# Four of eight experts in one wide pass, picked from 33 programs, and their output transposed back by DMA

## The chip, the cores and the metric

The kernel runs on one core of one Trainium2 chip. The metric is the device time of one execution in microseconds, the median of several runs of the same program. The profile comes from one further execution; its span, from the first to the last instruction, is a little shorter than the device time (270.0 us beside 271.8 us for that run). TensorE (PE in the profile, with its weight loads as PEld), VectorE (DVE), ScalarE (ACT), GpSimd (POOL) and SyncE (SP) have queues of their own [...]; 16 DMA engines move data beside them.

## What is computed

A block of the kind of Mamba 2 (chunked state space attention) gives 3072 tokens of 256 numbers. Each token then goes to one of eight experts. Only the second part, cut to its core, is touched by the change:

```python
def _moe_ref(x, w_gate, w1, w2):           # x 3072x256, w1 8x256x1024, w2 8x1024x256
    logits = x @ w_gate
    expert_idx = np.argmax(logits, axis=1)
    ...                                     # probs = softmax(logits)
    gate_w = probs[np.arange(N), expert_idx]
    for e in range(E):
        mask = expert_idx == e
        xe = x[mask]
        h = np.maximum(xe @ w1[e], 0.0)
        out[mask] = gate_w[mask, None] * (h @ w2[e])
```

With the inputs of the reference the experts get 372, 343, 418, 417, 336, 365, 415 and 406 tokens. The kernel may not know these counts; it finds them on the chip.

## The kernel before

Everything is fp32, with tokens along the free axis in the first layer. The routing puts each token's row (256 numbers, 8 logits, its number: `W` = 265) into `x_hbm`, where every expert has a stretch of `NR` rows. The first 17 of 24 token tiles are placed during the attention part, the last seven (`late`) between the matmuls of the experts. Rows that no token fills have to be zero and carry a token number that is out of range, so that their output is dropped: `empty(e)` writes them from `zrows`.

The expert part has two passes. The first takes 256 rows (`CA`) of each of the eight experts. The second takes what is beyond them, experts in pairs: 128 rows of each, and up to 64 more of each in one half tile. For the second pass the largest count of the pair chooses one of five programs, 128 + 16c columns wide:

```python
def up(xT, w, f, n, pp, step=CA):                    # first layer, one of 8 blocks of h
    p = pp.tile([128, 512], FP32, name="h_ps", tag="h", bufs=4)
    for i in range(0, n, step):
        for t in range(KT):                          # KT = 2
            c = t * F + f * 128
            nc.tensor.matmul(p[:, i:min(i + step, n)], lhsT=w[:, c:c + 128], rhs=xT[:, t, i:min(i + step, n)],
                             start=(t == 0), stop=(t == KT - 1))
    return p[:, 0:n]

def m_y(e, hT, xs, gt, mo, pp, between=None, scalar=True, last=False):   # second layer, 128 tokens
    p = pp.tile([128, DM], FP32, name="y_ps", tag="y", bufs=2)
    for f in range(FT):                              # FT = 8
        nc.tensor.matmul(p, lhsT=hT[:, f], rhs=w_sb[e][1][:, f * DM:f * DM + DM], start=(f == 0),
                         stop=(f == FT - 1))
        ...
    put(p, xs, gt, mo, scalar, last)                 # scale by the gate, send rows to out by their numbers

for v in range(E // 2):                              # second pass
    ...
    for c in tc.Switch(cls[v], 5, f"p{v}"):
        for i in range(2):
            m_h(2 * v + i, pr[v]["xT"][i], pr[v]["hT"][i], 128 + 16 * c, pp)
        if c:
            m_half(v, mo, pp)                        # the two halves share one 128-row result
    send(yh, pr[v]["xh"][:, 0])
    ...                                              # hint of the next switch, rows of the next pair
    for i in range(2):
        m_y(2 * v + i, ...)
```

The hidden layer comes out of `up` with its features on partitions and goes into `m_y` as the stationary operand, so that the output rows have tokens on partitions and can be scattered. The first layer needs the rows transposed. VectorE splits the fp32 rows into 16-bit halves (`halves`, L651), a DMA transposes them (L653), and VectorE joins them again (`words`, L658):

```python
def halves(tiles):
    ...
    for i, xs in enumerate(tiles):
        f = xs.bitcast(U16).rearrange("p (j c) -> p c j", c=2)
        for t in range(KT):
            nc.vector.tensor_copy(pl[:, i, :, t], f[:, :, HB * t:HB * t + 128])
    tt = ea.tile([128, TA + 1, 2, KT, 128], U16, name="plT", bufs=2)[:, 0:n]
    nc.sync.dma_start_transpose(out=tt..., in_=pl...)
    return tt
```

Weights of all eight experts (2 MB each: `w1` and `w2`) have buffers of their own and are loaded once, in order, by SyncE's queue, ahead of their use; they stay for the second pass.

## Time and profile before

| | |
|---|---|
| device time, median of 3 runs | 271.53 us (270.83 to 271.98) |
| span of the profile | 270.0 us |
| first matmul of the experts | 83.2 us |
| first pass of the eight experts | 83.2 to 194.6 us |
| second pass, four pairs | 194.6 to 262.8 us |
| last seven tiles placed by GpSimd | 119.7 to 149.3 us |
| rows of the second pass first read | 167.2 us |
| DMA | 43.57 MB, mean 161 GB/s |

The page shows for each engine its busy time, then the span in 40 slices of 6.75 us with the busy share in tenths. A row of a group names the line of the source, the engine, the operation and the tiles (output<-input), how often it ran, its busy time and mean duration; behind the second bar stands the time for which its engine had been idle before it, and what ended that. The chain of waits follows the work that ended last backwards from the end, step by step, to what released each. Where a step is a matmul, the stretch from its start to the next is TensorE's own pace. SPq is SyncE issuing DMAs: their data move later. Every source matmul in fp32 shows as two instructions, so 64 instructions `h_ps` are the 32 matmuls of a pair.

### The profile page before, as it was taken

What the parts mean: (1) busy time and instruction counts of PE and PEld (TensorE: products, weight loads), DVE (VectorE), ACT (ScalarE), POOL (GpSimd) and SP (SyncE); (2) the same over time, 40 slices, a digit from 0 to 9 for tenths busy, and PEclk for the clock granted to TensorE, in tenths of its full rate; (3) what the DMA queues carried; (4) which work ended last, traced back from release to release, by engine and by line L of the source; (5) the groups of instructions that cost most, each with busy time, mean ns of one, the idle gap of its engine ahead of it and who ended that gap; (6) DMA issues with size and microseconds to landing.
All of it is one profiled execution on the core that took longest, in us unless ns stands there. A gap on an engine that the chain in (4) does not pass through costs nothing.

```text
span 270.0 us, 7603 instructions
## 1 busy us (share of the span) xinstructions
PE 252.9 (94%) x3044; PEld 213.7 (79%) x3067; DVE 110.7 (41%) x358; ACT 104.5 (39%) x304; POOL 87.0 (32%) x171
## 2 busy tenths in 40 slices
PE   8799898999997999999999999999999999999990
PEld 2577677677776888888888888888998978989770
DVE  4889887888854240421211111233225115321010
ACT  6958574655543423223232323141050520604200
POOL 5666875866720002025504120202211102121021
PEclk9999999999999999999999999999999999999996
DMA  6956767671434899949695959533330601401010
GB/s 182 374 172 171 228 199 236 165 247 51 135 118 101 212 367 310 384 177 294 236 256 202 279 199 335 130 91 78 103 85 9 94 4 30 90 6 40 2 35 28
DMA packets 29715, 43.57 MB, mean 161 GB/s; under 512 B 16203, under 2 KB 19917, under 8 KB 27984
## 3 DMA queue, kind: packets, MB, share of 16 engines
q1 hardware_dynamic: 27152, 36.32, 45.4%
q0 software_dynamic: 2496, 6.41, 7.1%
q8 instruction: 36, 0.59, 0.9%
q14 instruction: 31, 0.25, 0.3%
HBM read 29.10 MB, written 10.73 MB: 147 GB/s over the span
## 4 chain that ended last, share of the span: by engine, by line
PE 82%; DVE 5%; DMA 4%; issue 4%; POOL 2%; ACT 1%; POOLq 0%; ACTq 0%; DVEq 0%
PE h_ps L685 33%; PE y_ps L720 30%; PE y L176 5%; PE rows_ps L176 4%; PE g L176 3%; PE A L176 3%; PE yh_ps L731 3%; DVE L L359 2%; DMA x_hbm<-rows,pos 1%; DMA xs<-x_hbm 1%; DMA az<-in_az_dram 1%; DMA ct<-in_CT_dram 1%; DVE M L386 1%; PE rank L176 1%; DVE S L431 1%
## 5 line engine op out<-in xcount | busy, mean ns | idle before, releaser
L685 PE MATMUL h_ps<-xT,w 128*128 128x256 f32 (+3 forms) x516 | 90.3, 334 | 0.6 <-ACT xT L641 0.5
L685 PEld LDWEIGHTS h_ps<-xT,w 128*128 128x128 f32 x516 | 81.3, 190 | 8.2 <-ACT xT L641 0.7
L720 PE MATMUL y_ps<-w,hT 128*128 128x256 f32 x384 | 84.9, 380 | 0.0
L720 PEld LDWEIGHTS y_ps<-w,hT 128*128 128x128 f32 x384 | 72.6, 190 | 10.5 <-issue 0.8
L696 ACT ACTIVATE hT<-h_ps 128x256 f32<-128x256 f32 (+3 forms) x128 | 43.3, 339 | 60.8 <-PE h_ps L685 53.1
L711 POOL DMA_INDIRECT out_dram<-yo,xs x24 | 23.7, 988 | 91.1 <-ACT yo L703 64.7
L553 POOL DMA_INDIRECT x_hbm<-rows,pos x24 | 24.4, 1015 | 20.6 <-DMA x_hbm<-zrows 13.3
L359 DVE TENSOR_TENSOR_SCAN L<-abc,ident 128x512 f32<-128x512 f32 x24 | 29.1, 1213 | 0.0
L651 DVE COPY pl<-xs 128x256 uint16<-128x256 uint16 x44 | 10.4, 298 | 43.8 <-DMA xs<-x_hbm 43.7
L658 DVE COPY xT<-plT 128x512 uint16<-128x512 uint16 (+1 forms) x30 | 10.6, 415 | 33.6 <-DMA plT<-pl 27.8
L703 ACT ACTIVATE yo<-y_ps,gate 128x256 f32<-128x256 f32 x14 | 6.6, 474 | 39.4 <-PE y_ps L720 24.5
L386 DVE TENSOR_TENSOR M<-g,L 128x512 f32<-128x512 f32 x24 | 16.5, 687 | 5.6 <-PE g L176 5.1
L176 PE MATMUL rows_ps<-turn,yT 128*128 128x136 f32 x96 | 15.4, 283 | 3.5 <-issue 2.7
L705 DVE TENSOR_SCALAR yo<-y_ps,gate 128x256 f32<-128x256 f32 x10 | 4.8, 482 | 29.3 <-PE y_ps L720 29.3
L176 PE MATMUL g<-ctm,bt 32*64 32x128 f32 x384 | 16.3, 280 | 0.5 <-ACT ctm L293 0.4
L176 PEld LDWEIGHTS rows_ps<-turn,yT 128*128 128x128 f32 x96 | 14.5, 192 | 1.3 <-issue 0.4
L711 POOL DMA_INDIRECT out_dram<-yh,xh x4 | 3.9, 978 | 35.7 <-ACT yh L733 23.9
L470 ACT COPY rows<-rows_ps 128x264 f32<-128x264 f32 x24 | 9.1, 380 | 13.5 <-PE rows_ps L176 10.9
L176 PE MATMUL y<-M,xn 64*32 64x64 f32 x768 | 12.9, 223 | 1.2 <-issue 1.2
L457 ACT COPY yT<-y 128x256 f32<-128x256 f32 x24 | 8.9, 372 | 12.2 <-PE y L176 10.2
L176 PEld LDWEIGHTS g<-ctm,bt 32*64 32x64 f32 x384 | 10.4, 131 | 3.2 <-ACT ctm L293 0.9
L366 POOL TENSOR_TENSOR bs<-bn,L 128x128 f32<-128x128 f32 x22 | 9.0, 410 | 11.1 <-DVE L L359 10.0
(132 smaller groups left out, 203.3 us busy)
## 6 DMA issues: line engine op xcount, KB each, us to landing
w<-in_w_dram SPq DMA_DIRECT2D x13, 1024.0 KB
x_hbm<-zrows SPq DMA_DIRECT2D x8, 463.8 KB
xn<-in_x_dram SPq DMA_DIRECT2D x12, 256.0 KB
w<-in_w_dram SPq DMA_DIRECT2D x12, 256.0 KB
xs<-x_hbm SPq DMA_DIRECT2D x8, 265.0 KB
ct<-in_CT_dram SPq DMA_DIRECT2D x6, 256.0 KB
bt<-in_BT_dram SPq DMA_DIRECT2D x6, 256.0 KB
bn<-in_B_dram SPq DMA_DIRECT2D x6, 256.0 KB
```

Of the source, the lines that this page charges most:

```text
L176: i = nc.tensor.matmul(out, lhsT=lhsT, rhs=rhs, **kw)
L359: nc.vector.tensor_tensor_scan(out=s["L"].rearrange("p h i -> p (h i)"), data0=s["abc"], data1=ident8.rearrange("p h i -> p (h i)"), initi ...
L366: nc.gpsimd.tensor_tensor(out=bs[n % 2], in0=gr[n // CG]["B"][:, n % CG].rearrange("p (h m) -> p h m", h=8), in1=bc(st[n]["L"][:, :, CH - ...
L386: nc.vector.tensor_tensor(out=s["M"].rearrange("p (s v u) i -> p s v (u i)", s=2, v=2), in0=s["g"][:, :, 0:256].rearrange("p v (s f) -> p ...
L470: nc.scalar.copy(out=rt[g][:, k - R0[g], 0:DM + E], in_=p)
L553: s_ = nc.gpsimd.indirect_dma_start(out=x_hbm[:, :], out_offset=bass.IndirectOffsetOnAxis(ap=pos[:, k:k + 1], axis=0), in_=rt[grp[k]][:, k ...
L651: nc.vector.tensor_copy(pl[:, i, :, t], f[:, :, HB * t:HB * t + 128])
L658: nc.vector.tensor_copy(xT.bitcast(U16).rearrange("p t (j c) -> p c t j", c=2), tt)
L685: nc.tensor.matmul(p[:, i:min(i + step, n)], lhsT=w[:, c:c + 128], rhs=xT[:, t, i:min(i + step, n)], start=(t == 0), stop=(t == KT - 1))
L696: nc.scalar.activation(hT[:, f, 0:n], p, func=ACT.Relu)
L711: s_ = nc.gpsimd.indirect_dma_start(out=out[:, :], out_offset=bass.IndirectOffsetOnAxis(ap=xs[:, TOK:TOK + 1].bitcast(I32), axis=0), in_=y ...
L720: nc.tensor.matmul(p, lhsT=hT[:, f], rhs=w_sb[e][1][:, f * DM:f * DM + DM], start=(f == 0), stop=(f == FT - 1))
```

## The change

Experts 0 to 3 keep their two passes. Experts 4 to 7 get one pass over all their rows, up to 512 (`CP`), by a program of the width that the count asks for, in steps of 8 from 256 to 512: 33 programs (`NCP`) for each of four experts. The aim is to spend no columns on rows that only fill tiles. So that the width of both layers can follow the count, the second layer has the weights stationary and the tokens streaming; its result has features on partitions, and a DMA transpose turns it back. The one-pass experts stand between the layers of the others, so that transposes and loads have a whole layer of matmuls beside them. Since a one-pass expert needs all its rows, all tokens are placed at the start of the expert part, and the zero rows behind the tokens (`empty_last`) are written once the final counts are known. The one-pass experts share two sets of weight buffers.

```diff
+EP = 4
+CP = 512
+NCP = (CP - CA) // 8 + 1
-NR = N + 128
+NR = N + CP
+    def empty_last(e):
+        r = nc.values_load(nk[0:1, E + 1 + e:E + 2 + e], engines=[ENG.SP], ...)
+        d = nc.sync.dma_start(out=x_hbm[ds(r + e * NR, CP), :]..., in_=zrows)
+    def p_load(e):
+        xs = ea.tile([128, CP // 128, W], FP32, name="xp", bufs=2)
+        nc.sync.dma_start(out=xs, in_=x_hbm[e * NR:e * NR + CP, :].rearrange("(t p) w -> p t w", p=128))
     ...
+    def m_one(e, hT, yT, n, pp):
+        for f in range(FT):
+            nc.scalar.activation(hT[:, f, 0:n], up(ex[e]["xT"], w_sb[e][0], f, n, pp, CP), func=ACT.Relu)
+        for m in range(KT):
+            p = pp.tile([128, 512], FP32, name="y_ps", tag="y", bufs=2)[:, 0:n]
+            for f in range(FT):
+                c = f * DM + m * 128
+                nc.tensor.matmul(p, lhsT=w_sb[e][1][:, c:c + 128], rhs=hT[:, f, 0:n], start=(f == 0),
+                                 stop=(f == FT - 1))
+            nc.scalar.copy(yT[:, m, 0:n], p)
+    def turn_back(yT):                    # halves by VectorE, transpose by DMA: 16 blocks
+        ...
+    def put_back(e, tt, mo):
+        for i in range(CP // 128):
+            yo = mo.tile([128, DM], FP32, name="yo", bufs=4)
+            nc.vector.tensor_copy(yo..., tt[:, i])
+            nc.vector.tensor_scalar(out=yo, in0=yo, scalar1=ex[e]["gate"][:, i:i + 1], ..., op0=ALU.mult)
+            send(yo, ex[e]["xs"][:, i])
     ...
+        def new_w(e):
+            w_sb[e] = [w2pool.tile([128, KT * F], FP32, name=f"wp{u + 1}", bufs=2) for u in range(2)]
+        def late():                       # in the middle of the first layer of expert 0
+            g_in(0)
+            empty(2)
+            empty(3)
+            load_w(1, (1,))
+            rank_pe(last, rank_ps)
+            rank(last)
+            for k in range(R0[GA], NT):
+                place(k)
+                nc.gpsimd.memset(apart, 0.0)
+            x_words(1)
+            g_in(1)
+            over(tb, pp)                  # the final counts and the programs
+            for e in range(EP, E):
+                empty_last(e)
+            new_w(EP)
+            load_w(EP)
+            p_load(EP)
+        def one(i):
+            e = EP + i
+            hT = mo.tile([128, FT, CP], FP32, name="hTp", bufs=1)
+            for c in tc.Switch(cls[i], NCP, f"e{e}"):
+                m_one(e, hT, yTp, CA + 8 * c, pp)
+            hint(i + 1)
+            return turn_back(yTp)
+        first(0, late)
+        ...
+        first(1)
+        second(0, pick)
+        x_halves(EP)
+        ...                               # rows of 2 and 5, weights of 2 and 5
+        second(1, pick)
+        x_words(EP)
+        ...
+        tt = one(0)
+        x_words(EP + 1)
+        put_back(EP, tt, mo)
+        first(2)
+        ...                               # rows of 3 and 6, weights of 3 and 6
+        tt = one(1)
+        x_words(EP + 2)
+        put_back(EP + 1, tt, mo)
+        second(2, pick)
+        ...                               # rows and weights of 7
+        tt = one(2)
+        ...
+        first(3)
+        ...                               # rows of the pairs (0,1) and (2,3) beyond 256
+        tt = one(3)
+        put_back(EP + 3, tt, mo)
+        second(3)
+        ...                               # second pass of the pairs (0,1) and (2,3), as before
```

Functions `first` and `second` are the two layers over 256 rows as before; in the changed source `halves` transposes at L678, `words` copies at L683, `place` stands at L568.

## The prediction

> **What bounds the kernel now.** I read the busy table and the slices first, then the groups, then the chain of waits, and last the timeline of the places that the change touches. The page says which engine is full and from where:

> ```profile
> PE 252.9 (94%) x3044; PEld 213.7 (79%) x3067; DVE 110.7 (41%) x358; ACT 104.5 (39%) x304; POOL 87.0 (32%) x171
> PE   8799898999997999999999999999999999999990
> DMA  6956767671434899949695959533330601401010
> L685 PE MATMUL h_ps<-xT,w 128*128 128x256 f32 (+3 forms) x516 | 90.3, 334 | 0.6 <-ACT xT L641 0.5
> L720 PE MATMUL y_ps<-w,hT 128*128 128x256 f32 x384 | 84.9, 380 | 0.0
> ```

> From the 13th slice on (6.75 us each) TensorE stands at 9 in every slice, and the two expert layers (L685, L720) wait for nothing: 0.6 and 0.0 us of idle time. The expert part is bound by matmuls alone. A duration of 380 ns is the time through the array and not the spacing; the chain gives the spacing:

> ```profile
> 94.88 0.20 PE rank L176 x8
> ...
> 97.76 6.91 PE y_ps L720 x32
> ...
> 194.56 7.14 PE h_ps L685 x64
> ...
> 208.61 9.55 PE h_ps L685 x64
> 218.17 3.60 PE yh_ps L731 x32
> ...
> 243.10 8.95 PE h_ps L685 x64
> ```

> Each fp32 matmul of the source is two instructions. 256 columns cost 6.91/32 = 215.8 ns, 176 columns 9.55/64 = 149.2 ns, 128 columns 7.14/64 = 111.6 ns. So a column costs (215.8-149.2)/80 = 0.83 ns, an instruction some 2.5 ns more, and weight loads hide even at 128 columns. The expert part runs from 83.2 us to 262.8 us, where the last output is scaled; 7.2 us of tail follow.

> [...] the last matmul ends near 262.8, and the clock column halves at about 266:

> ```profile
> 265.00:266.00 1.00, 0.00 (x0) 0.00 (x0) 0.00 (x0) 0.00 (x0) 0.13 (x1) 0.93 0.34 115
> 266.00:267.00 1.00, 0.00 (x0) 0.00 (x0) 0.00 (x0) 0.00 (x0) 0.00 (x0) 0.50 0.09 25
> ```

> (the third number from the end is the clock). [...] the transpose that SyncE handed over at 101.07 moved its 256-byte rows only between 106 and 109 us, behind weights and zero rows issued before it. [...] Here the four switches come with hints a layer ahead, and TensorE lost at most 0.17 us before one of them, so 33 programs instead of 5 should cost little.

> **The change, part by part.** *Matmul work of experts 4 to 7.* From the reference's inputs the experts get 372, 343, 418, 417, 336, 365, 415 and 406 tokens; the programs of 128, 176, 128 and 160 columns in the trace fit this. Before: first pass 4 x 2 x 6.91 = 55.3 us; second pass, first layer 7.14 + 8.95 = 16.1; its second layer 64 instructions x 215.8 = 13.8; the halves of 6 and 7, 3.6. Sum 88.8. After: programs of 336, 368, 416 and 408 columns, 64 instructions each, at 282.5, 309.2, 349.2 and 342.5 ns: 1283.4 x 64 = 82.1 us. **Gain: 6.6 us**, nearly all because rows round up to 8 and not to 256 + 128 (+64). This is the whole possible gain, 2.4%; experts 0 to 3 keep their work.

> *Small costs on TensorE.* The count (L569) now stands right behind the ranking in one PSUM tile and must wait for VectorE to read it: about 0.5 us. Six switches for four, and waits where one layer of a wide program hands over to the next: about 0.5 us. Together **+1 us**.

> *Added work beside the path.* 16 more VectorE passes per expert for turning back and scaling (some 0.3 to 0.45 us each, as L651 and L658 show), about 5 us per 18 to 22 us of matmuls, on an engine that is 41% busy. The 16 output copies of the one-pass experts leave ScalarE. Hidden.

> *Moved: the placing of the last seven tiles and expert 4's rows.* This is what I think decides. Before, the second pass's rows were read at 167 us, long after they were placed (119 to 149 us). Now expert 4's one pass needs all its rows as soon as experts 0 and 1 have run: 83.2 + 4 x 6.91 + 0.7 = **111.5 us**. The rows' way there, first two lines of the chain (start, us, what was waited for):

> ```profile
> 75.55 3.50 DMA x_hbm<-rows,pos
> 79.07 2.96 DMA xs<-x_hbm
> ```

> then a transpose of 8 blocks and the copy that waits for it, from the timeline:

> ```profile
> 84.52 1.36 SPq L653 DMA_TRANSPOSE plT<-pl  x1
> 89.43 0.79 DVE L658 COPY xT<-plT 128x512 uint16<-128x512 uint16 x2 [3.21 <-DMA plT<-pl]
> ```

> and a line of the list of waits, and the row by windows of a stretch in which DMA is full (its last number is GB/s):

> ```profile
> POOL x_hbm L553 <- DMA x_hbm<-zrows: 13.3, 1, 13.3
> 110.00:114.00 4.00, 4.00 (x20) 3.53 (x19) 1.99 (x13) 1.25 (x4) 0.00 (x0) 1.00 1.03 414
> ```

> Placing waits for the zero rows of the experts still to be emptied. Before, the last of these were written late, hence the 13.3 us; now only those of experts 2 and 3 count, which are down at about 90.8 (the read at 90.75 waited for them). Seven placings at 1.3 us (119.72, 121.09, 122.39 in the timeline) end at about 100; each lands 3.5 us after its start (first line of the chain), so at 103.5. Meanwhile the SyncE queue gets w2 of expert 1 (1.05 MB), the four new fills (4 x 0.54 MB) and w of expert 4 (2.1 MB), and the placings add 0.95: 6.3 MB at 0.4 MB per us (414 GB/s) end at about 106.5. The read of 512 rows goes behind them: landed at 108 to 109.5 (two reads of half its size took from 79.07 to 83.6). Eight copies (0.9 us per four) 1.8 us; transposes of 16 blocks instead of 8, 5 to 5.5 us (8 took 84.52 to 89.43); three copies back 1.2 us. Expert 4 can begin at 116 to 118: **a wait of 4 to 7 us, taken as 5.5**. It is longer than the 3.3 us after which the clock halved[...]: **+2 us**.

> *Later hand-overs.* Expert 6's rows (third one pass) go into the buffer of expert 4's rows, which is free only when expert 4's outputs are sent. Counted from the end of expert 4's program: turning back 7.5 us, scaling and sending 8, read 3, weights of 3 and 6 (4.2 MB) 10.5, transposes behind them and copies 5: 34 us. TensorE has 6.9 + 19.8 + 6.9 + 0.9 = 34.5 us of work there. This is a draw; I put **+1 us**.

> Sum: -6.6 + 1 + 5.5 + 2 + 1 = +2.9 us, 274.4 us.

> **The rivals.** *A: the rows come in time.* Then only the matmul sum counts: -6.6 + 1 = -5.6 us, 266 us. For it: the schedule puts two experts between placing and need, and DMA is not full in every slice. Against it: the chain above has no slack, and before, the 512 rows of a pair had 18 us and more. With a wait below 3 us and no clock loss it is 268 to 269.

> *B: DMA becomes the bound of the whole middle.* The one pass streams weights through two buffers, each refilled only after its expert is done, and transposes queue behind 4 MB of weights (10.5 us). If such a wait comes at three hand-overs at 3 us[...], the time is 280 or more. For it: the 34 against 34.5 us. Against: weights of one expert are 5 us against 18 to 22 us of matmuls.

> *C: instruction fetch.* [...] if hints fail, each of four wide switches and its way back cost 1 to 2 us (an estimate from the 3.5 us that SyncE waits at its own last branch, L983, part of it a register load), up to +10. The 0.17 us of before speak against it.

> **Range and chances.** My sum is 274.4. The lower end, 268, is rival A with a short wait; the upper, 281, is B in part. Faster by over 2% means below 266.1, which needs nearly the whole matmul gain and no wait: 0.04. Slower by over 2% means above 277, with the waits at their upper ends or one more clock loss: 0.32. The rest, 0.64, is within 2%.

> **What would show it.** In the profile after: matmuls of 336 to 416 columns with 64 instructions per expert in 18.1, 19.8, 22.3 and 21.9 us (right or wrong to 0.2 us for the gain); an idle TensorE between about 111 and 117 us, ended by VectorE's copy of the transposed rows (L683), and a clock below 1 in the slice after it; the third one pass waiting for the same copy, or not. I am wrong downwards if the placed rows are read before 100 us; wrong upwards if TensorE shows idle time at each of the one-pass experts, or "issue" of over 1 us at the switches.

## Result, and the profile after

The changed kernel takes **297.15 us** (median of 4 runs, 296.86 to 297.71) against 271.75 us for the kernel before on the same chip: a ratio of 1.094, 95% interval 1.090 to 1.098. It is 25 us slower where 3 us were predicted, and above the predicted range of 268 to 281 us.

The page after, in the lines that answer to those shown of before (busy table, slices of 7.4 us, granted clock, DMA, the two first-layer groups):

```profile
PE 257.4 (87%) x2843; PEld 187.9 (64%) x2843; DVE 120.9 (41%) x381; ACT 96.6 (33%) x269; POOL 93.3 (32%) x188
PE   7899999999989990699999968799999980999990
PEclk9999999999999997599999997999999997599997
DMA  6966776624449985994526993590651043301010
L709 PE MATMUL h_ps<-xTp,wp 128*128 128x336 f32 (+3 forms) x128 | 45.7, 518 | 15.2 <-DVE xTp L683 13.3
L709 PE MATMUL h_ps<-xT,w 128*128 128x256 f32 (+2 forms) x260 | 49.3, 352 | 9.2 <-ACT hT L720 8.7
```

Before, TensorE stood at 9 in every slice from the 14th to the 39th. Now there are three dents, at slices 16 and 17 (0 and 6), 24 to 26 (6, 8 and 7), and 33 and 34 (8 and 0); the granted clock falls to 7 and 5, to 7, and to 7 and 5 in or right after them. DMA stands at 9 through one slice of the first two and at 3 or 4 in the third. The idle time moved into the expert layers: 15.2 us ahead of the one-pass experts' first layers, 9.2 ahead of the others'. The timeline of TensorE places them (start, us, what; in brackets the idle time before and what ended it):

```profile
120.62 11.16 PE L709 MATMUL h_ps<-xTp,wp 128*128 128x336 f32 x32 [9.32 <-DVE xTp L683]
...
147.77 10.06 PE L709 MATMUL h_ps<-xTp,wp 128*128 128x368 f32 x32
...
178.61 7.55 PE L709 MATMUL h_ps<-xTp,wp 128*128 128x416 f32 x16 [3.98 <-DVE xTp L683]
188.01 5.85 PE L709 MATMUL h_ps<-xTp,wp 128*128 128x416 f32 x16 [1.85 <-issue]
...
251.41 8.52 PE L709 MATMUL h_ps<-xT,w 128*128 128x128 f32 x48 [8.70 <-ACT hT L720]
```

Expert 4 waits 9.3 us and then takes 11.16 us for a layer that takes 9.31 at full clock (*One program*, below). Expert 5 starts with no gap. Expert 6 waits 4.0 us, loses 1.7 to the clock (7.55 us for its first 16 instructions, 5.85 for the next) and stops again for 1.85. Expert 7 has no gap. Pair 0 waits 8.7 us, and its 48 instructions take 8.52 us instead of 5.62 (*Late put-back*, below). Sum: 9.3 + 1.85 + 4.0 + 1.7 + 1.85 + 8.7 + 2.9 = 30.3 us of waits and half clock. With the gain of 6.3 (below) that makes +24.0 of the 25.4 us measured; 1.4 is left for the small costs.

The chain of waits shows how expert 4's rows came (what was waited for, from when and how long), and ScalarE's timeline what happened at expert 6:

```profile
105.17 2.94 DMA out_dram<-yo,xs
108.12 5.15 DMA xp<-x_hbm
115.03 4.39 DMA plT<-pl
```

```profile
184.01 0.47 ACT L727 ACTIVATE yo<-y_ps,gate 128x256 f32<-128x256 f32 x1 [15.74 <-PE h_ps L709]
...
187.44 1.75 ACT L753 ACTIVATE hTp<-h_ps 128x416 f32<-128x416 f32 x4 [2.18 <-issue]
```

The last placing starts at 100.05 and the rows are read at 108.12. The chain names an output (`out_dram`) as what the read waited for, but in the packet records the outputs' rows move until 110.5, after the read has started; those of the last placing move until 107.35, just before it. The read waited for the placing. At expert 6 ScalarE stands 15.7 us at the output copies of expert 2 (`yo`). The name in the bracket misleads: those products were long done. What was missing is a free `yo` tile, for VectorE and GpSimd fill and send the same four tiles with expert 5's outputs until 184.0. The relus of expert 6 stand behind, and TensorE has four product tiles to run ahead. Another 2.2 us lie between ScalarE's exponential, done at 185.26, and its first relu at 187.44, with no cause in the profile ("issue"); the fetch of its program, below, is the likely one.

**Theory at this point**: three separate waits, of different causes, each made dearer by the clock: the rows of expert 4, the order of transfers and the shared output tiles at expert 6, and at pair 0 queues standing behind the late outputs of expert 7. **Rivals**: one common cause, so that a wait taken away comes back at the next hand-over; or the fetch of the 33 programs.

### The profile page after: what moved, and what is told of

Read it like the earlier page. It is cut to its first block, busy times and chain, and to the rows that moved or that the text cites. A ratio compares the mean times of both kernels' runs of the same rounds, so it can differ in the third digit from the quotient of the medians.

```text
span 295.4 us, 7232 instructions
## 1 busy us (share of the span) xinstructions
PE 257.4 (87%) x2843; PEld 187.9 (64%) x2843; DVE 120.9 (41%) x381; ACT 96.6 (33%) x269; POOL 93.3 (32%) x188
## 4 chain that ended last, share of the span: by engine, by line
PE 64%; DMA 14%; DVE 8%; issue 5%; POOL 5%; ACT 1%; POOLq 0%; DVEq 0%; ACTq 0%
PE h_ps L709 28%; PE y_ps L758 12%; DMA plT<-pl 8%; PE y L179 6%; PE g L179 4%; PE y_ps L744 4%; PE A L179 3%; PE rows_ps L179 3%; POOL x_hbm L568 3%; PE abc L179 2%; DMA xp<-x_hbm 2%; DVE L L373 1%; DMA xs<-x_hbm 1%; PE yh_ps L784 1%; DVE pl L676 1%
## 5 line engine op out<-in xcount | busy, mean ns | idle before, releaser
L709 PE MATMUL h_ps<-xTp,wp 128*128 128x336 f32 (+3 forms) x128 | 45.7, 518 | 15.2 <-DVE xTp L683 13.3
L709 PE MATMUL h_ps<-xT,w 128*128 128x256 f32 (+2 forms) x260 | 49.3, 352 | 9.2 <-ACT hT L720 8.7
L735 POOL DMA_INDIRECT out_dram<-yo,xp x16 | 16.5, 1034 | 116.0 <-DVE yo L776 113.3
L709 PEld LDWEIGHTS h_ps<-xT,w 128*128 128x128 f32 x260 | 44.0, 206 | 14.3 <-ACT hT L720 9.7
L709 PEld LDWEIGHTS h_ps<-xTp,wp 128*128 128x128 f32 x128 | 25.9, 204 | 33.8 <-DVE xTp L683 14.1
L744 PE MATMUL y_ps<-w,hT 128*128 128x256 f32 x192 | 42.4, 380 | 0.0
L758 PE MATMUL y_ps<-hTp,wp 128*128 128x336 f32 (+3 forms) x128 | 41.7, 484 | 0.0
L744 PEld LDWEIGHTS y_ps<-w,hT 128*128 128x128 f32 x192 | 36.3, 190 | 5.7 <-issue 0.7
L758 PEld LDWEIGHTS y_ps<-hTp,wp 128*128 128x128 f32 x128 | 24.3, 190 | 16.7 <-issue 10.0
L720 ACT ACTIVATE hT<-h_ps 128x256 f32<-128x256 f32 (+2 forms) x64 | 20.5, 342 | 35.5 <-PE h_ps L709 24.3
L568 POOL DMA_INDIRECT x_hbm<-rows,pos x24 | 24.3, 1012 | 12.7 <-DVE gate L649 5.9
L683 DVE COPY xT<-plT 128x512 uint16<-128x512 uint16 (+1 forms) x14 | 4.9, 409 | 23.3 <-DMA plT<-pl 23.0
## 6 DMA issues: line engine op xcount, KB each, us to landing
xn<-in_x_dram SPq DMA_DIRECT2D x12, 256.0 KB
w<-in_w_dram SPq DMA_DIRECT2D x12, 256.0 KB
ct<-in_CT_dram SPq DMA_DIRECT2D x6, 256.0 KB
```

The source lines that it names most:

```text
L568: s_ = nc.gpsimd.indirect_dma_start(out=x_hbm[:, :], out_offset=bass.IndirectOffsetOnAxis(ap=pos[:, k:k + 1], axis=0), in_=rt[grp[k]][:, k ...
L720: nc.scalar.activation(hT[:, f, 0:n], p, func=ACT.Relu)
L735: s_ = nc.gpsimd.indirect_dma_start(out=out[:, :], out_offset=bass.IndirectOffsetOnAxis(ap=xs[:, TOK:TOK + 1].bitcast(I32), axis=0), in_=y ...
L758: nc.tensor.matmul(p, lhsT=w_sb[e][1][:, c:c + 128], rhs=hT[:, f, 0:n], start=(f == 0), stop=(f == FT - 1))
```

## Experiments

### Pair 0: which queue stands behind expert 7's outputs

The page names GpSimd's zeroing of the pair's hidden tiles as what ScalarE waited for. *Zeroing first*: `second(3)` and the zeroing of pair 0's tiles ahead of the put-back.

```diff
-        put_back(EP + 3, tt, mo)
-        b_gates(0)
         second(3)
+        pr[0]["hT"] = [new_hT(mo) for _ in range(2)]
+        for h in pr[0]["hT"]:
+            nc.gpsimd.memset(h[:, :, 144:CB], 0.0)
+        put_back(EP + 3, tt, mo)
+        b_gates(0)
```

> The changed kernel with the second layer of expert 3 and the two clearing writes of the first pair's hidden tiles moved ahead of the sending of expert 7's output; the gates of the pairs stay behind it. In the changed kernel TensorE stands idle 8.70 us before the first pair's layer and then runs 48 matmul instructions in 8.52 us instead of 5.4 us. Theory 'clearing on GpSimd' (the wait that the profile names: GpSimd clears only after it has sent expert 7): wait and half clock go, 297.1 - 11.9 = 285 us. Theory 'one of several' (ScalarE's exponentials for the pairs' gates wait for VectorE, which is behind the same sending, until 250.6 us, while the clearing ended at 251.0): the wait stays, 296 to 297 us, and the wait is then put down to VectorE or ScalarE.

Measured: 300.81 us, ratio 1.110 (1.104 to 1.115). The zeroing is done by 248, and pair 0 still waits 9.9 us, now for ScalarE's last gate exponential at 256.0, which needs VectorE, which stands behind the put-back. So GpSimd was one of several queues held, and taking it away alone brings nothing. That the run is 3.7 us slower than the changed kernel comes from ahead of the edit: its profile has some 2.8 us more of waits and half clock at expert 6 and 1.1 us more at expert 4, which shows how much these vary.

*Late put-back*: expert 7's outputs are put back after pair 0's first layer, which takes them out of the way of all three queues.

```diff
         tt = one(3)
-        put_back(EP + 3, tt, mo)
 ...
             send(yh, pr[v]["xh"][:, 0])
+            if v == 0:
+                put_back(EP + 3, tt, mo)
```

> The changed kernel with one line moved: expert 7's output is scaled and sent only after the first layer of the first pair. That frees GpSimd, VectorE and ScalarE together. Theory 'one of several': the 8.70 us and the 3.2 us at half clock go, 297.1 - 11.9 = 285 us, with the pair's layer starting at about 242 us. If instead the pair's rows or the program fetch were the true cause, the wait stays near 8 us.

Measured: 286.61 us, ratio 1.057 (1.053 to 1.062), 10.5 us less by moving one line. Of the wait 0.85 us stays and the 48 instructions take 5.62 us. The put-back waits for a DMA transpose; whatever stood behind it in VectorE's, ScalarE's or GpSimd's order waited too.

### Expert 6: order of transfers, then output tiles

*Weights first*: the weights of experts 3 and 6 ahead of expert 6's rows, which can't be read until expert 4's outputs are sent.

```diff
         a_load(3)
-        p_load(EP + 2)
         load_w(3)
         new_w(EP + 2)
         load_w(EP + 2)
+        p_load(EP + 2)
```

> The changed kernel with the weights of experts 3 and 6 issued before the read of expert 6's rows instead of behind it. Theory 'transposes behind weights in the queue': expert 6's transposes (162.6 us) then have a free queue and land at about 168 instead of 177, the 4.0 us wait of TensorE before expert 6 and most of its 2 us at half clock go; the inner wait of 1.85 us (ScalarE's output copies wait for the output buffers that expert 5's rows hold) stays or grows to 3: 291 to 293.5 us. Theory 'the buffer': the rows of expert 6 wait for the sending of expert 4 in any case, and the order of the weights changes nothing: 296.5 to 297.5 us.

Measured: 296.16 us, ratio 1.092 (1.087 to 1.098). TensorE:

```profile
176.24 5.75 PE L709 MATMUL h_ps<-xTp,wp 128*128 128x416 f32 x16
185.78 8.49 PE L709 MATMUL h_ps<-xTp,wp 128*128 128x416 f32 x16 [3.79 <-ACT hTp L753]
```

From the handing over of expert 6's transposes to the copy of the turned rows (L683) pass 5.8 us now (167.51 to 173.30) and passed 14.5 before (162.63 to 177.09), so the weights ahead of them did delay them. Expert 6 starts with no wait. But that alone does not show the edit to be the reason: in four runs that leave this order as it was, expert 6 waits 3.5 us (zeroing first), 0.9 (late put-back), 0.7 (weights behind rows, below) and 0 (the clock run, below). And it now runs into a full set of product tiles, waits 3.8 us there for ScalarE and goes on at half clock: a hidden wait took the place of the open one, and the gain of 1 us is no more than the spread of the runs.

*Tiles apart*: to this, output tiles of the two-pass experts of their own.

```diff
     def put(p, xs, gt, mo, scalar=True, last=False):
-        yo = mo.tile([128, DM], FP32, name="yo", bufs=4)
+        yo = mo.tile([128, DM], FP32, name="ys", bufs=2)
```

> The changed kernel with the weights of experts 3 and 6 issued ahead of the rows of expert 6 (as in the run before that did this alone) and, added to it, output tiles of the two-pass experts apart from those of the one-pass experts (2 of their own, beside the 4). Output-buffer theory: the wait inside expert 6 (1.85 us in the changed kernel, 3.79 us with the weights first alone) came from ScalarE standing at the output copies of expert 2 until the outputs of expert 5 had been sent, so it falls under 0.5 us, expert 6's first layer runs at full clock (11.2 us), and the time falls from 296 to about 289-291. Rival (ScalarE is held by something else there, such as its gates' exponentials behind VectorE's queue): the inner wait stays at 3 to 4 us and the time at 296.

Measured: 291.69 us, ratio 1.072 (1.065 to 1.078).

```profile
178.54 11.34 PE L709 MATMUL h_ps<-xTp,wp 128*128 128x416 f32 x32
```

Expert 6's first layer runs through at full clock. A smaller wait, 1.5 us by ScalarE, shows inside expert 5; it comes back below. The time is 0.7 us above the 289 to 291 expected. Whether the tiles would have done it without the order was not run.

### Do the waits add?

The three edits together: weights first, tiles apart, late put-back.

> The two edits of the run above, and expert 7's outputs put back after pair 0's first layer. If the waits before expert 6 and before pair 0 are separate and simply add, the time is that of the run above minus 10.5 us: 279-281, of which the wait before expert 4 is still 9.5 us and its half clock 2 us. Rival (they share a cause, and taking one away moves the wait to the next hand-over): 284-287, the time of the late put-back alone.

Measured: 280.81 us, ratio 1.035 (1.029 to 1.040).

```profile
121.08 12.23 PE L709 MATMUL h_ps<-xTp,wp 128*128 128x336 f32 x32 [9.18 <-DVE xTp L683]
...
238.26 5.62 PE L709 MATMUL h_ps<-xT,w 128*128 128x128 f32 x48 [0.86 <-ACT hT L720]
```

They add: 291.7 - 10.5 = 281.2, and expert 6 runs through from 177.1 with no gap. The rival of one common cause falls for expert 6 and pair 0. The largest wait left is that before expert 4 with its clock: 9.2 + 2.9 us.

### Expert 4: the clock

40 matmuls whose result is not used fill the wait of the changed kernel.

```diff
+        for _ in range(40):
+            p = pp.tile([128, 512], FP32, name="keep_ps", tag="y", bufs=2)
+            nc.tensor.matmul(p, lhsT=kz[:, 0:128], rhs=kz, start=True, stop=True)
         tt = one(0)
```

> The changed kernel with 40 idle-work matmuls (bf16, 128x512, their result unused) on TensorE between the second layer of expert 1 and expert 4, in the wait of 9.3 us. Clock theory: the half-speed stretch after the wait is the price of TensorE standing still, so expert 4's first layer takes its 32 x 282.5 = 9.04 us instead of 11.16 us, nothing else moves, and the time falls by about 2 us, to 295. Rival (the first matrices of expert 4 are slow for a reason of their own, such as fetching its program or reading fresh weights): still 11.2 us, and the time stays at 297. If the 40 matmuls take longer than the wait, expert 4 starts later than 120.6 us and the gain is smaller.

Measured: 294.52 us, ratio 1.081 (1.073 to 1.089), 2.6 us less.

```profile
111.67 9.12 PE L1051 MATMUL keep_ps<-kz 128*128 128x512 bf16 x40
121.34 9.28 PE L709 MATMUL h_ps<-xTp,wp 128*128 128x336 f32 x32 [0.56 <-DVE gate L649]
```

The layer takes 9.28 instead of 11.16 us at nearly the same starting time, which is 1.9 of the 2.6; the rest is no more than noise. In this run the slow stretch goes with TensorE standing still (9.32 us before the layer there, 0.56 here), and neither with fresh weights nor with the fetch of a program, which both stayed.

### Expert 4: the rows

*Weights behind rows*: in the changed kernel, the 2 MB of expert 4's weights are asked for after its rows.

```diff
+            p_load(EP)
             new_w(EP)
             load_w(EP)
-            p_load(EP)
```

> The changed kernel with the weights of expert 4 issued behind the read of its rows instead of ahead of it. In the changed kernel the last of the seven placings starts at 100.05 and the rows are read at 108.1, 8 us later, where 3.5 us were expected. Theory 'placings share the DMA engines with the bulk of the other queue': without 2 MB of weights they land by 104 to 105, the rows are there 4 us sooner, the wait before expert 4 falls from 9.3 to 4 to 5.5 us: 291.5 to 293.5 us. Rival 'placings are slow of themselves or wait for the fills': the read stays at 107 to 108 and the weights now come later, so 297 us or more.

Measured: 295.29 us, ratio 1.089 (1.085 to 1.094). The chain:

```profile
100.22 4.34 DMA x_hbm<-rows,pos
104.78 4.71 DMA xp<-x_hbm
111.43 8.51 DMA plT<-pl
```

The last placing lands after 4.3 us instead of 8, and the rows are there 3.8 us earlier; the transposes then queue behind the weights and take 8.5 instead of 4.4 us. The wait before expert 4 is 9.6 us, where 4 to 5.5 were expected: what is put behind the 2 MB pays for them.

*Placing earlier*: with the three edits, the zero rows of experts 2 and 3, for which the placings wait, are asked for with those of 0 and 1.

```diff
             if n == 21:
-                for e in range(2):
+                for e in range(4):
                     empty(e)
 ...
             g_in(0)
-            empty(2)
-            empty(3)
```

> The kernel of the three edits (weights 3 and 6 ahead of expert 6's rows, output tiles apart, expert 7's outputs late; 280.8 us, wait before expert 4 9.2 us) with the emptying of experts 2's and 3's rows asked for ten chunks earlier, so that GpSimd's last seven placings need not wait for it and start at about 89 us instead of 92.9. Theory that the wait before expert 4 is one chain from the placings on (placing, landing, rows read, pieces, transposes, words): everything behind moves up by the same 4 us, the wait falls to about 5.2 us, the time to 276.5-277.5. Rival (the landing of the placings is set by the hardware queue that is full of expert 4's weights, issued at 95.7-97.9, not by when they are issued): the rows are read at 109.5-110 as before, the wait stays at 9 us and the time at 281.

Measured: 280.66 us, ratio 1.039 (1.034 to 1.044).

```profile
96.88 8.77 DMA x_hbm<-rows,pos
105.86 4.63 DMA xp<-x_hbm
112.25 6.55 DMA plT<-pl
```

Neither theory was right. The rows are read 4.1 us earlier, as the chain theory said. But the transposes, starting earlier, meet more weights and take 2.2 us longer; and expert 0's rows land later (TensorE waits 1.7 us for them ahead of the expert part). The wait falls by 0.8 us only and the time not at all.

*Expert 2's first layer ahead of expert 4*, with the halves of experts 2 and 3 each a place earlier (the diff only reorders the calls `first`, `second`, `one` and the loads):

> The changed kernel with expert 2's first layer run ahead of expert 4 (the halves of experts 2 and 3 each move up by one place, so that experts 4, 5, 6, 7 are followed by second(2), first(3), second(3) and pair 0), the second matrix of expert 4 behind its transposes, weights ahead of rows for experts 6 and 7, and expert 7's outputs after pair 0's first layer. Theory that the wait before expert 4 is only the rows' lateness: 18 us of other work ahead of expert 4 covers it, no wait above 1 us and full clock there, the wait before pair 0 is gone, and what stays is the wait inside or before expert 6 (2-4 us) : 272-277. Rival (the wait is set by the hardware queue being full of weights, so that what is asked for earlier only lengthens it): the transposes of expert 4 land behind the weights of expert 2 and a wait of 5 us or more stays before expert 4: 280-288.

Measured: 307.43 us, ratio 1.136 (1.130 to 1.142), the slowest of all, and a fault of my order: the transposes of expert 2 stand in SyncE's queue behind the read of expert 4's rows, and the read behind the placings (the read is handed over at 109.24 us, the transposes from 109.72 on). TensorE waits 6.5 us before expert 2 and 4.1 before expert 4, and ScalarE's late relus come back inside experts 5 and 7 and at pair 0. It says nothing on the theory, and the question is asked again below.

*Rows turned on TensorE*: in place of pieces, DMA transposes and words (1.7 + 6.6 + 1.5 us in the run with earlier placing), eight transposes of 128x128 on TensorE.

```diff
-        x_halves(EP)
 ...
         second(1, pick)
-        x_words(EP)
+        ex[EP]["xT"] = ea.tile([128, KT, CP], FP32, name="xTp", bufs=1)
+        for t in range(CP // 128):
+            copy = nc.scalar.copy if t % 2 else nc.vector.tensor_copy
+            copy(ex[EP]["xT"][:, :, 128 * t:128 * t + 128], xT_of(ex[EP]["xs"][:, t], pp, "h", 4))
```

> The kernel of the run above, and expert 4's rows turned on TensorE (8 transposes, copied out by VectorE and ScalarE in turn) in place of the pieces on VectorE, the DMA transposes and the words, which took 1.9 + 4.3 + 1.5 us of the chain. Chain theory: about 5.5 us less before expert 4, whose wait falls to 0-1 us with expert 4 at full clock; the time is 268-270, one per cent below the kernel before (271.5), because then only the matmul gain of 6.6 us and small waits are left. Rival (a wait taken away here comes back at the next hand-over, as with the weights first): 272-276, with waits of 2 us or more at experts 5 to 7. If the placings' landing did not move up, the wait is about 4 us and the time 274.

Measured: 278.37 us, ratio 1.031 (1.026 to 1.035). *And the second matrix of expert 4 behind its rows* (`load_w(EP, (0,))`, `p_load(EP)`, `load_w(EP, (1,))`):

> The kernel of the run above with the second matrix of expert 4 asked for after its rows instead of before. Queue theory (rows and placings queue up behind weights in flight): the rows of expert 4 are read 1-2 us earlier and land 1-2 us faster, so a wait that was left before expert 4 falls by 2-3 us, to nothing; time 267-269. Rival: the second matrix now lands too late, and a wait of 1-5 us appears in the middle of expert 4 (at its second layer), time 270-274.

Measured: 277.31 us, ratio 1.028 (1.024 to 1.032). Of this one, TensorE:

```profile
111.13 1.04 PE L657 MATMUL xT_ps<-ident,xp 128*128 128x128 f32 x8
115.38 12.28 PE L709 MATMUL h_ps<-xTp,wp 128*128 128x336 f32 x32 [3.21 <-issue]
```

Both times lie far above what was expected (268 to 270 and 267 to 269). The rows are there when TensorE comes (no idle time before the transposes), and they are turned and copied out by 112.3. Yet 3.2 us of "issue" follow, 5.6 us in the run before: TensorE waits for nothing that the profile shows. Something lay hidden under the wait for rows.

### Under the wait: the fetch of the program

The packet records show packets of kind "instruction", 16 KB each on one queue; their times fit TensorE's programs. In the changed kernel three come at 105.2, 108.6 and 112.1 us, all while TensorE is at work or waits for rows. With the rows turned on TensorE the one before expert 4 comes only at 115.9 and at 112.6 us, in both runs 3.7 to 3.9 us after the rows have landed (112.1 and 108.9), and expert 4 starts 2.8 us after it. My reading: the switch stands behind transposes that wait for the rows, and is not reached before. Two runs tell this from late data. *One program*: expert 4's choice is left out; the 336-column program, which these inputs choose, stands in the code.

```diff
-            for c in tc.Switch(cls[i], NCP, f"e{e}"):
-                m_one(e, hT, yTp, CA + 8 * c, pp)
+            if i == 0:
+                m_one(e, hT, yTp, 336, pp)
+            else:
+                for c in tc.Switch(cls[i], NCP, f"e{e}"):
+                    m_one(e, hT, yTp, CA + 8 * c, pp)
 ...
-        hint(0)
```

> The kernel of the run before (three edits, fills early, expert 4's rows turned on TensorE, its second matrix behind its rows; 277.3 us, 3.2 us before expert 4 put down to 'issue') with expert 4's choice among 33 programs left out: its 336-column program, the one these inputs choose, stands straight in the code. Fetch theory (the 3.2 us are TensorE's fetch of the chosen program, which can't be asked for before the transposes ahead of the switch are through, and which had been hidden in the 9 us wait of the changed kernel): the wait falls to under 1 us, expert 4's first layer runs at full clock (9.1 instead of 12.3 us), the time falls by 5 to 6 us to 271-272.5. Rival (the copies of the turned rows or the landing of the first matrix hold it): 3 us of wait stay and the time is 276-278.

Measured: 271.61 us, ratio 1.005 (1.003 to 1.008).

```profile
116.09 9.31 PE L709 MATMUL h_ps<-xTp,wp 128*128 128x336 f32 x32 [0.37 <-ACT xTp L1043]
```

The wait and the half clock are gone. What the edit takes away is the switch as a whole; that its cost is the fetch rests on the packets. (The profiled execution took 273.65 us, with half clock ahead of the experts' first matrices, so its start, some 3 us late, is not to be compared.) *Rows turned inside the program*, so that the switch stands ahead of the transposes and the choice is kept:

> The same kernel with the choice kept and expert 4's transposes moved into the chosen program, behind the switch, copied out by ScalarE alone, so that the program can be fetched while expert 1's second layer runs. Fetch theory: the wait before expert 4 is only that for the rows and copies, under 2 us, and its first layer is at or near full clock: 271-274. Rival as above: no change from 277.

Measured: 278.52 us, ratio 1.032 (1.027 to 1.036). TensorE's packets come at 103.0 and 110.5 us, the first ahead of the rows (landed at 108.2), and it transposes at 110.44. But ScalarE, which copies out, goes through the same switch:

```profile
116.46 0.92 ACT L1022 COPY xTp<-xT_ps 128x256 f32<-128x256 f32 x3 [4.86 <-issue]
```

A packet of 8 KB comes at 114.7, 1.8 us ahead of this copy. The expectation (271 to 274) missed the number; the fetch that no longer held TensorE now held ScalarE, by this reading, for 4.9 us.

### Both layers of expert 2 ahead, in a better order

Rows by DMA and all choices kept; expert 2's rows, transposes and weights asked for ahead of the read that waits for the placings; `first(2)` and `second(2)` ahead of `one(0)`, `first(3)` between 4 and 5, `second(3)` between 5 and 6, tiles apart, late put-back, each next expert's `x_words` ahead of `turn_back`.

> Expert 2's both layers run ahead of expert 4 once more, this time with its rows, its turning and its weights asked for ahead of the wait for the placings (in the earlier try they stood behind that wait), the first layer of expert 3 between experts 4 and 5, its second between 5 and 6, nothing between 6 and 7, each next expert's rows turned back into words before the expert's outputs are turned, output tiles apart, expert 7's outputs after pair 0's first layer; expert 4's second matrix behind its rows; rows still turned by DMA and the choice of programs kept. If the wait before expert 4 is its rows' and its program's lateness and nothing more, 14 us of other TensorE work covers both: no wait above 1 us and no half clock at expert 4, waits of 0-1.5 us at experts 5 to 7, and the time is 266-269, below the kernel before (269-271.5). Rival (what is taken from one hand-over comes back at the next, because the queues of DMA and ScalarE are then the bound): 272-280, with 3 us or more at experts 5, 6 or 7.

Measured: 286.87 us, ratio 1.056 (1.052 to 1.061).

```profile
125.09 4.68 PE L709 MATMUL h_ps<-xTp,wp 128*128 128x336 f32 x16
131.96 4.79 PE L709 MATMUL h_ps<-xTp,wp 128*128 128x336 f32 x16 [2.19 <-ACT hTp L753]
...
213.00 7.44 PE L709 MATMUL h_ps<-xTp,wp 128*128 128x408 f32 x16 [3.15 <-ACT hTp L753]
...
240.25 7.51 PE L709 MATMUL h_ps<-xT,w 128*128 128x128 f32 x48 [7.07 <-ACT hT L720]
```

The 9 us before expert 4 are gone, at full clock, with TensorE's program and the rows both in time: that wait was lateness. But the time lies above even the rival's 272 to 280: 2.2, 3.2 and 7.1 us, all at ScalarE, came up elsewhere. Last, *ScalarE's exponentials behind its switches* (`g_out` of a one-pass expert after its own program, pair 0's gates ahead of `turn_back` of expert 7, pair 1's after pair 0's layer, the hint of expert 4's program after `first(2)`):

> The kernel of the run before (expert 2 ahead; 286.9 us, no wait before expert 4, but 2.2 us inside expert 4, 3.2 us inside expert 7, 7.1 us inside pair 0, each by ScalarE) with what ScalarE had to do ahead of its switches moved behind the one-pass programs: each one-pass expert's gate exponentials after its own program, pair 0's gates worked out ahead of expert 7's turning back, pair 1's after pair 0's layer, and the hint of expert 4's program after expert 2's first layer. ScalarE theory (it reaches its switch late because its exponentials wait for VectorE's turning-back copies, and fetches its program only then): pair 0's wait falls under 1 us with full clock (-9 us), expert 7's under 1 us with full clock (-4 us), expert 4's to about 1 us; the time is 270-273, that of the kernel before. Rival (ScalarE's program fetch takes its 5 us from wherever it starts, and TensorE's four buffers of products cover only 4.7 to 5.7 us of it): the waits at experts 4 and 7 stay at 2 to 3 us, only pair 0's goes, and the time is 277-279.

Measured: 281.57 us, ratio 1.046 (1.041 to 1.052). Pair 0's wait falls to 3.8 us and expert 7's to 1.4 + 1.1; the 2.2 us inside expert 4 are gone, but its rows were late by 2.5 us this time, which gave ScalarE that much more time. ScalarE still comes to its programs late:

```profile
128.71 1.66 ACT L753 ACTIVATE hTp<-h_ps 128x336 f32<-128x336 f32 x4 [5.54 <-issue]
```

5.5 us at expert 4, 4.4 at expert 7, 4.8 at expert 5 lie between ScalarE's last operation ahead of a switch and its first behind it. TensorE covers 4.7 to 5.8 us of that with the four product tiles, so it shows only where ScalarE comes late. Both theories had a part, and the time is above both (270 to 273, 277 to 279). No version ran below the kernel before, the one without expert 4's choice included.

## Why the prediction was wrong

**The matmul gain held.** Start to start and without waits, the one-pass experts take 18.2 us (expert 4, from the run with one program), 20.1, 22.35 and 21.9 us (from the run with three edits): 82.5 against 82.1 predicted, a gain of 6.3 us.

**The small costs** (+1) held roughly: 1.4 us are left in the sum, the 0.4 us behind the ranking among them. Two readings were off without harm: TensorE stands at 9 only from the 14th slice on (the 13th is at 7), and of the three starts read as placings, the second is an output. The placings ran 1.26 us apart, against 1.3 taken.

**The first wait was the right step, mis-sized**: 9.3 us instead of "4 to 7, taken as 5.5". Of its terms the landing of the last placing failed: 3.5 us taken from a quiet stretch, 8 measured. I let the placings and 2 MB of weights share the DMA and end at 106.5, but did not let the placing itself stand behind the weights. With the weights behind the rows it landed in 4.3 us. So the rows, read at 108.1, were there at 113.3 instead of 108 to 109.5; pieces (1.7), transposes (4.4) and words (1.2) were near the estimates. **The clock loss** of +2 was an estimate that no trace of before shows; for this wait it was right (1.85).

**The later hand-overs (+1) failed in size**: 34 against 34.5 us, "a draw", became 4.0 us and 1.7 of clock in the profile of the changed kernel (0 to 3.5 us of wait in the four other runs with this order). The count left out the transfers' order (the weights of 3 and 6 behind a read that waits) as something that holds the transposes up, 14.5 us instead of 5.8. And it looked at rows only: the other 1.85 us at expert 6 went with output tiles of their own, which the count had nowhere.

**"Hidden" failed**, and it is the largest miss: VectorE's added passes and the output copies were put beside the path because VectorE was 41% busy before (it is 41% busy after, too) and ScalarE lost work. At pair 0 that cost 8.7 + 2.9 us. What counted was not the 5 us of added work but that it waited for a DMA, and with it what stood behind it in its engine's order. I counted engine time, not what stands behind it. Moving one call took it away (0.85 us left of the 8.7, and no half clock).

**Rival B** (waits at three hand-overs, 280 and more) is what happened, but not by its reason: in the idle times themselves DMA was busy 60% before expert 4 and 31% before pair 0, and full only before expert 6. I had said I would be wrong upwards if every one-pass expert showed idle time; two of the four did, and a pair.

**Rival C** (fetch) seems refuted by the changed kernel's profile, since experts 5 and 7 start with no gap; by my reading of the packets it was covered. The runs give sizes: 2.8 us from packet to first matmul on TensorE, 4.4 to 5.5 us between ScalarE's last operation ahead of a switch and its first behind it, 6 us with the clock at expert 4 once the rows are in time (3.2 us of wait and 3.0 of half clock, gone but for 0.37 us with one program). "33 programs instead of 5 should cost little" was true only under other waits.

What stays open: the run with one program has waits of 0.4, 0.9, 0.9 and 0.7 us, 1.0 us of transposes, and some 1 to 1.5 us from emptying rows earlier; with 6.3 us gained and 1.4 of small costs that should be 0 to 0.5 us above the kernel before, and it is 1.5 us above (0.5%). About 1 us was not found.

## What to carry to other kernels

An engine that is less than half busy can still stop others if an operation in its order waits for a transfer (VectorE was 41% busy, and pair 0 waited 8.7 us with the put-back ahead of it, 0.85 without): ask of each added operation what stands behind it, and put work that only feeds an output behind the next layer's. When a transfer landed went here with what was handed to the DMA ahead of it (the last placing landed after 4.3 us without 2 MB of weights, after 8 with them), so measure it in the stretch where it will run; moving it earlier may only hand the queueing to the next transfer (rows read 4.1 us earlier, transposes 2.2 us longer). And a gain of 2% from finer shapes, bought with 33 programs, has to pay for its long waits (here for each of 3.6 us and more, up to 9.9) twice, once as idle time and once as clock.

## What the runs showed of the hardware

In these runs the length of an idle time alone did not say whether it cost the clock. The first line below, from the clock run, follows 3.10 us of idling and is at half clock in part; the second, from *Zeroing first*, follows 3.50 us and is not (both are 16 instructions that take 5.75 to 5.85 us):

```profile
184.36 7.55 PE L709 MATMUL h_ps<-xTp,wp 128*128 128x416 f32 x16 [3.10 <-ACT hTp L753]
179.85 5.85 PE L709 MATMUL h_ps<-xTp,wp 128*128 128x416 f32 x16 [3.50 <-DVE xTp L683]
```

Behind eight transposes that needed late rows, the first instruction packet ahead of expert 4 came at 112.6 and 115.9 us instead of 105.2, though the hint of it was given in the layer before; that a program is sent for only at its switch is my reading of these times and was not shown apart. And two queues met in the DMA: the last placing issued by GpSimd landed 4.3 us after its start without, and 8 to 9.3 us with, 2 MB of weights handed over by SyncE before it.
